# Four interleaved attention layers on one core: exponentials of two and two PSUM banks, later loads in pieces, a new written order

## The chip, the cores and the metric

The kernel runs on one core of a Trainium2 chip. The metric is the device time of one execution in microseconds (us), lower is better. TensorE is called PE here, VectorE DVE, ScalarE ACT, GpSimd POOL, SyncE SP; PEld are PE's weight loads.

## The reference

The input x has 2048 rows of 512 columns in bf16. Four layers follow each other, A, B, A, B, with the same weights for both A and for both B. Each adds its result to x, and each starts with a layernorm without scale.

```python
# A: 32 heads of 16, causal window of 256 rows
q, k, v = split(layernorm(x) @ wqkv)
scores = where(0 <= i - j < 256, q @ k.T * 0.25, -1e9)
x = x + concat(softmax(scores) @ v) @ wo
# B: 32 heads of 16, linear attention
phi = lambda t: where(t > 0, t + 1, exp(t)) + 1e-6
kv, z = phi(k).T @ v, sum(phi(k))
x = x + concat((phi(q) @ kv) / (phi(q) @ z + 1e-6)) @ wo
```

## The kernel before

Rows of x are cut into 16 tiles of 128, and four tiles make a block of 512. For a block, layer A computes transposed queries and keys (`q_unit`, `k_unit`, L711 to L742) and values (`v_unit`, L743), each by `proj` (L510): four matmuls of 128x512 into one bank of PSUM, followed by one evacuation. The values go through SBUF to SBUF DMAs on SP's queue (L757, four for each tile) into a layout in which two heads stand apart. Layer B of the same block follows as soon as the block is there: keys, values and queries (`bk_unit`, `bv_unit`, `bq_units`), a running sum over the blocks, and after the last block of a layer the normalizers (`norm_pair`, `norm_unit`) and the output products (`p2_tile`). PSUM has 8 banks of 128x512 f32, all held as one tile `psb`.

Attention is made of 152 score operations (`scores`, L762), 76 for each layer A. One of them is 8 to 12 small matmuls of 32 rows (L774), which fill four banks: banks 0, 1 and 2, and one of the banks 3 to 7. ACT then takes the exponential of three banks in one instruction of 128x1536 (L785) and of the fourth in one of 128x512 (L788). DVE or POOL masks the edges (L803, L808), and groups of 128x34 matmuls (L831) multiply with the values. Since banks 0 to 2 exist once, the score matmuls of the next operation wait until the exponential of L785 has read them.

Which instruction comes when on every engine isn't left to a scheduler. `ORDER` (L207) is a string of some 2,350 entries. An entry is the number of an operation, a letter for the engine (P for PE, A for ACT, V for DVE, G for POOL, S for SP, H for a landing in memory) and the buffers or banks that it takes. `Planner.run` walks over it and emits. Operations that several engines can do, such as masks, evacuations and the layernorm's factors, are given to one by the letter. An entry with F puts matmuls of the identity into a free bank (`fill`, L442), whose results nobody reads; there are 113 of them.

The rows 8 to 15 of x, and the weights woA, wB and woB, are loaded by five large DMAs that ACT issues between its exponentials (L1051 to L1056). At the start ACT and DVE zero the five buffers of the spread values (L499, L501). At the end a check of the normalizers is reduced to one flag (L886, L1307, L1311), all engines read it (L1312), and a branch leads to a safe version that never runs with these inputs.

Of the kernel before, what the change touches and what calls it, by code (L numbers as in the profile page):

```python
# [9 lines left out]
ACT = mybir.ActivationFunctionType  # L10
# [7 lines left out]
P = 128  # L18
D = 512
# [5 lines left out]
VW = 17  # L25

# [93 lines left out]

class Planner:
# [22 lines left out]
    def run(self):  # L144
# [7 lines left out]
        ahead = {"P": 9, "A": 1, "V": 9, "G": 1}  # L152
        marks = {}
        for e, k in ahead.items():
            marks.setdefault([i for i, x in enumerate(plan) if x[1] == e][-k], []).append(engine[e])
        for i, (n, e, places) in enumerate(plan):
            for m in marks.get(i, ()):
                self.tc.mark_branch_hint_location("safe", "LikelyTaken", [getattr(mybir.EngineType, {"ACT": "Activation", "POOL": "Pool"}.get(m, m))])
# [54 lines left out]
109P 110P 107V 111P 112V 129P04 130A 292P6 293V 287P7 288V 66P5 67V 30A 31H 144P03 145A 297P6 298V 318P7 319V 320S 301P5
131A 132G 133G 146A 149P06 150A 311P7 548V0 127V 116V 134P4 139P3 135P 302V 560V1 151A 152V 549G 550V00 552V2 561G 553G
155P05 156A 136P 137P 312V 138V 140P 141P 157A 147G 159G 142P 160P06 161A 162A 164G 163V 303P5 175P07 176A 143V 554V1
555S 321P4 322V 323S 304V 305P6 153G 158G 306V 180P03 177A 181A 299P4 300V 556V0 154G 148G 165P7 166P 182A 170P5 186P06
167P 187A 178G 171P 172P 173P 188A 174V 562V1 168P 191P03 169V 185G 557G 551S 184G 324P4 192A 190G 183G 558V2 559S 563S
325V 189V 326S 193A 194G 2F6 327P05 328A 329A 825V0 307P6 308V 3F4 332P03 333A 195G 179G 201P7 202P 196P5 197P 203P 198P
199P 200V 821V1 209S0 334A 336G 337P04 338A 339A 204P 205V 569P6 341G 331V 1F5 342P03 343A 344A 822G 13V 571V 313P5 3F7
348P04 349A 579P7 330V 314V 350A 340G 353G 345G 3F3 364P03 365A 366A 346V 347V 581V 352V 206S1 351V 570V 817V2 369P04  # L220
371A 370A 215S2 212S3 335G 359P5 360P 361P 354P6 362P 363V 367G 818G 819V02 820S 26A 27H 355P 356P 357P 234V 580V 374P03
372V 829V2 375A 376A 378V 377G 368G 584P5 3F4 379P04 380A 585V 823V1 358V 381A 373G 830G 383G 826G 382G 309P7 3F3 385P03
386A 207P5 310V 384V 831V0 832S 586S 387A 390V 389V 388G 572P6 573V 401P04 402A 208V 574P7 575V 391P3 392P 393P 406P06
827V2 396P5 403A 404V 407A 397P 394P 398P 399P 408A 410G 576V 218V0 411P04 395V 412A 216P7 217V 230V1 413A 415G 219G
409G 405V 3F6 416P03 417A 418A 419G 420V 567P6 3F7 422P04 423A 568V 400V 414G 421G 424A 426V 425V 587P7 588V 589S 824S
213P3 438P05 439A 427G 2F6 433P6 434P 428P7 443P04 440A 444A 445A 447G 429P 430P 431P 435P 432V 436P 437V 442V 220V01
221S 448P05 449A 582P7 450A 451G 8V 446V 214V 828S 3F6 453P04 454A 564P6 566V 441V 452V 455A 456G 458G 457G 3F5 459P03
460A 593P5 565V 594V 461A 462V 463V 590P4 595S 591V 592S 596P06 597A 598A 464G 465P5 466P 467P 601P03 602A 468P 470P6
471P 603A 231G 472P 473P 606P04 605G 469V 599V 474V 604V 583V 607A 608A 609V 210P5 3F6 611P03 612A 610G 837P6 838V 613A
614V 616V 615G 600G 3F7 617P04 618A 833P7 834V 619A 620G 622V 621V 3F6 633P03 634A 475S1 476P6 232V0 477V 487V0 488G 28A  # L230
29H 478S0 623P7 484S2 211V 624P 638P04 639A 625P 626P 481S3 628P6 629P 630P 631P 640A 642G 643P05 644A 627V 226V1 849P7
850V 851S 635A 645A 647G 641G 636G 632V 852P4 853V 854S 648P07 839P3 649A 577P5 578V 650A 653V 646V 651V 840V 654P04
637V 655A 656A 658V 657V 489G10 652G 490S 479P6 485P5 670P07 671A 659G 2F3 665P4 666P 667P 672A 675P03 676A 673G 222V0
223G 224G1 668P 660P7 661P 662P 486V 663P 664V 680P05 480V 677A 681A 858P3 499V2 859V 225S 233S 860S 679V 669V 491V0
682A 684G 227G 683V 2F7 685P06 686A 687A 855P7 856V 3F5 691P03 692A 674V 689V 678V 693A 696V 695V 847P5 482P6 228G2 229S
690G 688G 707P04 708A 483V 694G 2F7 697P7 698P 702P6 709A 712P03 703P 713A 699P 700P 704P 705P 706V 717P04 714A 718A
495V1 496G 497G0 719A 721G 835P3 836V 701V 710V 848V 716V 2F6 722P06 723A 498S 724A 727V 725V 845P3 2F7 728P04 729A 500G
846V 492G 711G 726V 730A 267P5 3F7 861P06 862A 863A 275P7 276A 732V 715V 731G 720V 733G 734P4 735P 866P03 867A 739P6
740P 741P 277V 278V 736P 737P 738V 744S0 268A 747S1 857S 742P 872P07 743V 750S2 868A 871G 269V 870G 493G0 494S 873A
841P4 842V 270V 874A 875V 501G1 3F6 877P03 878A 843P6 879A 882G 844V 869V 3F7 883P04 884A 745P5 746V 3F6 897P03 865V  # L240
885A 886V 876G 748P5 749V 760V0 898A 864G 887P6 888P 902P04 889P 890P 880V 881V 756V1 757G 899A 758G02 903A 904A 751P5
752V 764V2 503V 891V 908P03 909A 239P70 240V 906G 910A 912G 235P50 236A 237V 913P04 914A 900G 892P3 893P 894P 895P 896V
915A 917V 918G 905V 238V 2F6 919P06 920A 921A 901G 502S 532P7 544P4 545A 951P03 952A 916G 911G 922V 907G 1F5 923P5 924P
928P6 546V 953A 547V 533A 925P 926P 927V 956P04 957A 955G 954G 958A 960G 961G 761G 929P 930P 931P 932V 534V 535V 263P5
264A 962P03 963A 245P61 246V 933P70 934V 253P42 254V 265V 266V 964A 967P06 969A 968A 753S1 754P7 241P61 242A 755V 768V1
769G 970G 249P52 250A 973P03 974A 972G 975A 243V 244V 251V 762G1 937P71 938V 252V 271P4 272A 965V 273V 274V 935P6 936V
247P7 987P05 989A 988A 990G 966V 976G 959G 255P30 504P51 505A 506V 248V 256A 259P40 260A 508P61 257V 258V 509A 759S
939P7 941A01 942G 940V 261P6 262V 763S 765A 507V 766V1 767S 992P03 994A 946V2 514P40 510P60 522P52 977P7 978P 979P 993A
997V 971G 995G 511A 980P 981V 943A 515A 512V 513V 523V 996G 991G 998P03 1000A 999A 518P42 944P7 519A 982P3 983P 984P
516P6 517V 1003P05 1005A 1004A 985P 986V 947A 524P60 773P51 1001V 520G 521V 1002V 945V 525A 526V 527V 770G1 528P30 529A  # L250
774A 775V 776V 1009P04 1010A 1011A 777P71 778A 530P6 536P3 779P50 780A 531V 787P62 771S 537A 788A 789V 790V 781V 782V
1012G 1013P7 1006G 1007G 538G 1008G 783P40 784A 1014P 1015P 1016P 1017V 791P62 785P5 786V 539V 948G 772V 1018P4 1019P
1020P 1021P 1022V 1041V 949P5 950A 793P70 1027P00 1028V 1023P11 809P5 794A 795V 796V 1024A 1029P0 1030V 1036A0 1025P1
# [75 lines left out]
def build(ctx, tc, A_x, A_wqkv, A_wo, B_x, B_wqkv, B_wo, out, force_safe=False):  # L329
# [95 lines left out]
    def fast_network(ctx_f):  # L425
# [934 lines left out]
```

## Time and profile before

| what | us |
|---|---|
| median of 3 timed runs | 447.42 |
| lowest and highest of them | 446.45 and 449.89 |
| the profiled execution's own time | 445.83 |
| its span, first to last instruction | 444.1 |

The profiled execution is 1.6 us under the median, and its span leaves 1.7 us around it. Busy time is the share in which an engine has an instruction in work; the records of two instructions that follow each other on ACT, DVE or PE can overlap, since one begins to read while the other still writes. Matmuls are pipelined: a 128x512 matmul has a record of 0.38 us, while the next starts after 0.22 us.

### The profile page before, as it was taken

The numbers are of one execution on the slowest core, as the hardware profiler recorded it, in microseconds if no ns is written. First come the engines' busy times: TensorE is split into PE (matmuls) and PEld (weight loads), VectorE is DVE, ScalarE is ACT, GpSimd is POOL, SyncE is SP. The second block draws the span as 40 slices with busy tenths as digits, with TensorE's granted clock in tenths as the row PEclk, the third lists the DMA queues.
The fourth block names the chain that finished last, engine by engine and source line by source line (L and its number), as shares of the span: only waits on it lengthen the run. The fifth ranks groups of instructions, "written<-read, shape, count | busy, mean of one in ns | idle before, by whom it ended". The sixth has DMA issues, their size and how long they took to land.

```text
span 444.1 us, 15303 instructions
## 1 busy us (share of the span) xinstructions
PE 423.7 (95%) x6307; PEld 223.3 (50%) x6307; DVE 367.3 (83%) x874; ACT 374.1 (84%) x474; POOL 219.7 (49%) x485
## 2 busy tenths in 40 slices
PE   7989989999999999999999999999999989999995
PEld 2346545555554646554344465554555555565332
DVE  6899897878677787768996988989887969789985
ACT  6879999999999999667689999999899989984631
POOL 5436555325554645523763374564255558543332
PEclk9999999999999999999999999999999999999999
DMA  7421331234203100001011015223511221100014
GB/s 235 134 76 33 79 85 27 51 69 139 50 17 65 35 13 15 13 3 49 0 39 30 18 23 86 38 27 63 74 38 40 39 38 27 38 3 2 2 47 146
DMA packets 54330, 22.27 MB, mean 50 GB/s; under 512 B 38384, under 2 KB 53744, under 8 KB 54256
## 3 DMA queue, kind: packets, MB, share of 16 engines
q1 hardware_dynamic: 49760, 16.80, 18.6%
q10 hardware_dynamic: 4496, 4.46, 3.5%
q8 instruction: 50, 0.82, 0.8%
q14 instruction: 24, 0.20, 0.1%
HBM read 6.29 MB, written 2.10 MB: 19 GB/s over the span
## 4 chain that ended last, share of the span: by engine, by line
PE 57%; DVE 16%; POOL 9%; ACT 7%; issue 6%; DMA 4%; SPq 1%; DVEq 0%; POOLq 0%; ACTq 0%
PE psb L520 32%; PE psb L831 11%; PE psb L774 7%; POOL pt L808 4%; ACT pt L785 3%; PE psb L444 3%; DVE pt L803 3%; DMA xnT<-xn 2%; ACT pt L788 2%; DVE pks L899 2%; DVE pqT L1037 1%; PE psb L539 1%; PE psb L1033 1%; POOL xn L607 1%; DVE vst L507 1%
## 5 line engine op out<-in xcount | busy, mean ns | idle before, releaser
L785 ACT ACTIVATE pt<-psb 128x1536 bf16<-128x1536 f32 (+1 forms) x152 | 218.2, 1435 | 18.8 <-PE psb L774 17.1
L808 POOL TENSOR_SCALAR_AFFINE_SELECT pt<-pt 128x256 bf16<-128x256 bf16 x274 | 113.6, 443 | 120.3 <-ACT pt L788 113.6
L788 ACT ACTIVATE pt<-psb 128x512 bf16<-128x512 f32 (+1 forms) x152 | 89.6, 593 | 2.0 <-PE psb L774 1.5
L831 PEld LDWEIGHTS <-pt 128*128 128x128 bf16 x2880 | 81.3, 96 | 18.0 <-issue 6.5
L831 PE MATMUL psb<-vbd,pt 128*128 128x34 bf16 x2880 | 86.5, 178 | 3.3 <-DVE qT L507 1.1
L520 PE MATMUL psb<-xnT,wA 128*128 128x512 bf16 x256 | 64.7, 380 | 1.6 <-DVE vst L507 0.8
L803 DVE TENSOR_TENSOR pt<-pt,tri 128x256 bf16<-128x256 bf16 (+1 forms) x149 | 55.1, 394 | 12.1 <-ACT pt L788 11.7
L774 PE MATMUL psb<-qT,kall 32*128 32x320 bf16 (+4 forms) x1568 | 60.7, 246 | 3.0 <-ACT pt L785 2.5
L520 PE MATMUL psb<-wB,xnT 128*128 128x512 bf16 x256 | 61.6, 380 | 1.6 <-DMA xnT<-xn 1.2
L520 PEld LDWEIGHTS <-xnT 128*128 128x128 bf16 x384 | 34.1, 97 | 41.8 <-issue 4.7
L774 PEld LDWEIGHTS <-kall 32*128 32x128 bf16 x1568 | 25.8, 92 | 45.6 <-issue 40.6
L520 PEld LDWEIGHTS <-wA 128*128 128x128 bf16 x256 | 21.9, 97 | 29.3 <-issue 9.1
L444 PE MATMUL psb<-identb 128*128 128x512 bf16 x113 | 33.0, 401 | 2.3 <-POOL identb L372 1.5
L520 PE MATMUL psb<-woA,oT 128*128 128x512 bf16 x128 | 32.7, 381 | 0.6 <-DMA oT<-o_sb 0.6
L520 PE MATMUL psb<-wA,xnT 128*128 128x512 bf16 x128 | 32.5, 380 | 0.5 <-DMA xnT<-xn 0.3
L520 PE MATMUL psb<-xnT,wB 128*128 128x512 bf16 x128 | 32.3, 380 | 0.0
L726 DVE TENSOR_TENSOR kall<-psb,eo 128x1024 bf16<-128x1024 f32 x24 | 29.1, 1213 | 3.3 <-PE psb L520 2.2
L520 PE MATMUL psb<-wkv,pqT 128*128 128x512 bf16 x128 | 30.4, 380 | 0.1
L845 DVE TENSOR_TENSOR o_sb<-psb,rall 128x256 bf16<-128x256 f32 x64 | 27.2, 424 | 2.4 <-DMA oT<-o_sb 0.2
L844 DVE RECIPROCAL rall<-psb 128x16 f32<-128x16 f32 x64 | 15.9, 249 | 15.8 <-PE psb L831 15.5
L641 DVE BATCH_NORM_STATS2 ln_st<-xres 128x6 f32<-128x512 f32 (+1 forms) x39 | 26.7, 684 | 1.4 <-DMA xres<-in_A_x_dram 1.0
L893 ACT ACTIVATE pks<-psb 128x512 bf16<-128x512 f32 x32 | 19.2, 603 | 5.9 <-PE psb L520 5.8
(126 smaller groups left out, 532.5 us busy)
## 6 DMA issues: line engine op xcount, KB each, us to landing
vbd<-vst SPq DMA_DIRECT2D x128, 34.0 KB, 1.9
out_dram<-ost SPq DMA_DIRECT2D x16, 128.0 KB, 1.8
xres<-in_A_x_dram ACTq DMA_DIRECT2D x1, 1024.0 KB, 6.0
wB<-in_B_wqkv_dram ACTq DMA_DIRECT2D x1, 1024.0 KB, 5.5
xnT<-xn SPq DMA_TRANSPOSE x40, 2.7
wA<-in_A_wqkv_dram SPq DMA_DIRECT2D x1, 512.0 KB, 6.8
xres<-in_A_x_dram SPq DMA_DIRECT2D x1, 512.0 KB, 8.0
wB<-in_B_wqkv_dram ACTq DMA_DIRECT2D x1, 512.0 KB, 3.8
```

Of the source, the lines that this page charges most:

```text
L444: nc.tensor.matmul(psb[:, k, :], lhsT=identb[:], rhs=identb[:].unsqueeze(1).to_broadcast([P, NCT, P]), start=True, stop=True)
L520: nc.tensor.matmul(t["t"][:], lhsT=lhs(c), rhs=rhs(c), start=(c == 0), stop=(c == NCT - 1))
L641: nc.vector.bn_stats(t["st"][:], x())
L726: nc.vector.tensor_tensor(kall[:, r0:r0 + 2, t, :, :, :].rearrange("p r m k h -> p r (m k) h"), ps().rearrange("p (r c) -> p r c", r=2).un ...
L774: nc.tensor.matmul(psb[:, sT.k + x if x < 3 else sS.k, at * 64:(at + w) * 64], lhsT=kbd[half(m)][32 * x:32 * x + 32, tt, m % 4, :, :], rhs ...
L785: nc.scalar.activation(body[:, 0:3, 0:w_all, :], psb[:, 0:3, 0:w_all * 64].rearrange("p x (s c) -> p x s c", c=64), ACT.Exp, scale=0.25)
L788: nc.scalar.activation(body[:, 3, 0:w_all, :], psb[:, sS.k, 0:w_all * 64].rearrange("p (s c) -> p s c", c=64), ACT.Exp, scale=0.25)
L803: nc.vector.tensor_tensor(v, v, mt, op=ALU.mult)
L808: nc.gpsimd.affine_select(out=v, in_=v, compare_op=ALU.is_ge, fill=0.0, base=1 if kind == 0 else -2, pattern=[[0, 4], [2 * sg, 64]], chann ...
L831: nc.tensor.matmul(t["O"][:, x, g, :, :], lhsT=parts[b][0][:, s0:s0 + 2, :], rhs=vbd[half(m)][:, m % 4, :, 4 * tt + g, :], start=(n == 0), ...
L845: nc.vector.tensor_tensor(o_sb[:, u0:u0 + nu, P * tt:P * tt + P].rearrange("p u (h e) -> p u h e", e=DH), Ov[:, :, :, 0:DH], r.to_broadcas ...
L893: nc.scalar.activation(dst(), ps()[:], ACT.Exp)
```

## The change

- **Exponentials.** The four banks of a score operation are split two and two: banks 0 and 1, and one of the pairs 2-3, 4-5, 6-7. Both exponentials have 128x1024 elements.
- **Loads.** The later parts of x come two tiles at a time, and the weights in halves of 256 columns. SP issues them instead of ACT, each at its place in the order.
- **Start.** POOL zeroes the five value buffers; before, ACT did two and DVE three. `spread` gets a second copy with zeros, and the block mask `bd`, f32 before, is bf16.
- **Normalizers.** The matmuls of `norm_unit` read all 128 rows of `hl`, against weights that are zero in the half that isn't meant; before, they read 64 rows at a tile position of their own.
- **End.** The flag is computed within the written order, ahead of the last outputs. Outputs can be put by ACT as well as SP (nine by ACT). The last tile of the order (tile 2) is computed and put in two halves of 256 columns.
- **Order.** All of `ORDER` is new; the program has 50 fill matmuls.

```diff
-            sT, sS = Slot(rings["ps"], 3, (0,)), Slot(rings["ps"], 1, (3, 4, 5, 6, 7))
+            sT, sS = Slot(rings["ps"], 2, (0,)), Slot(rings["ps"], 2, (2, 4, 6))
...
-                            psb[:, sT.k + x if x < 3 else sS.k, at * 64:(at + w) * 64],
+                            psb[:, sT.k + x if x < 2 else sS.k + x - 2, at * 64:(at + w) * 64],
...
-                nc.scalar.activation(body[:, 0:3, 0:w_all, :], psb[:, 0:3, 0:w_all * 64].rearrange("p x (s c) -> p x s c", c=64), ACT.Exp, scale=0.25)
+                nc.scalar.activation(body[:, 0:2, 0:w_all, :], psb[:, 0:2, 0:w_all * 64].rearrange("p x (s c) -> p x s c", c=64), ACT.Exp, scale=0.25)
...
-                nc.scalar.activation(body[:, 3, 0:w_all, :], psb[:, sS.k, 0:w_all * 64].rearrange("p (s c) -> p s c", c=64), ACT.Exp, scale=0.25)
+                nc.scalar.activation(body[:, 2:4, 0:w_all, :], psb[:, sS.k:sS.k + 2, 0:w_all * 64].rearrange("p x (s c) -> p x s c", c=64), ACT.Exp, scale=0.25)
...
-        for b, t, c, fn in ((b_x[8:NT], 15.0, 3.0, lambda e: load_x(nc.scalar, 8, NT - 8)),
-                            ([B("woA")], 19.0, 1.5, lambda e: nc.scalar.dma_start(woA[:], wcols(A_wo, 0))),
-                            ([B("wB", 1)], 22.0, 3.0, lambda e: nc.scalar.dma_start(wB[:, :, D:3 * D], wcols(B_wqkv, 1, 2))),
-                            ([B("wB", 0)], 27.0, 1.5, lambda e: nc.scalar.dma_start(wB[:, :, 0:D], wcols(B_wqkv, 0))),
-                            ([B("woB")], 70.0, 1.5, lambda e: nc.scalar.dma_start(woB[:], wcols(B_wo, 0)))):
+        def part(w, src, which, k):
+            return lambda eng: eng.dma_start(w[:, :, which * D + 256 * k:which * D + 256 * k + 256], wcols(src, which)[:, :, 256 * k:256 * k + 256])
+        for i in range(8, NT, 2):
+            load(b_x[i:i + 2], 11.0, lambda eng, i=i: load_x(eng, i, 2))
+        for k in range(2):
+            load([B("woA", k)], 14.0, part(woA, A_wo, 0, k))
+        for which in (1, 2, 0):
+            for k in range(2):
+                load([B("wB", which, k)], 18.0, part(wB, B_wqkv, which, k))
...
-                    nc.tensor.matmul(t["p"][:, n, :], lhsT=spread[r0:r0 + 64, 2 * j + n, :, :], rhs=hl[I // 2][r0:r0 + 64, :],
-                                     start=True, stop=True, tile_position=(r0, 0))
+                    nc.tensor.matmul(t["p"][:, n, :], lhsT=spread[:, I % 2, 2 * j + n, :, :], rhs=hl[I // 2][:], start=True, stop=True)
...
+            if final and i == LAST:
+                ost = slot("xn")
+                for k in range(2):
+                    c = slice(256 * k, 256 * k + 256)
+                    o, s, ps = proj(lhs, lambda n, c=c: rhs(n)[:, c], reads=reads, deps=deps, use=use, n=256)
...
+                if a == 1:
+                    nc.vector.tensor_reduce(vall, vflags, axis=AX.X, op=ALU.min)
...
 ORDER = """
-6G 5G 0G 2G 7V 14H 1G 3G 17H 4G 50A0 35V0 36G 15H 16H 45V1 46G 40V2 37V10 47V2 10F1 38P0 39A 9A 51V 41G 42V3 52P1 53V
...
```

Three places of the order follow. The first is ACT at the first exponentials of the program (`pt` are the exponentials' buffers, `vst` and `qT` evacuated values and queries), first before, then now.

```order
L507 CAST vst_137<-psb 128x32x16
L785 ACTIVATE pt_146<-psb 128x3x512
L788 ACTIVATE pt_146<-psb 128x512
L785 ACTIVATE pt_147<-psb 128x3x512
L358 DMA xres<-in_A_x_dram 128x8x512
L785 ACTIVATE pt_148<-psb 128x3x448
L788 ACTIVATE pt_147<-psb 128x512
```

```order
L584 ACTIVATE ln<-ln 128x1
L810 ACTIVATE pt_145<-psb 128x2x512
L813 ACTIVATE pt_145<-psb 128x2x512
L810 ACTIVATE pt_146<-psb 128x2x512
L813 ACTIVATE pt_146<-psb 128x2x512
L813 ACTIVATE pt_147<-psb 128x2x448
L810 ACTIVATE pt_147<-psb 128x2x448
```

Three banks and one have become two and two, and the load is gone from ACT. The second place is SP's queue in the first third of the program (`vbd<-vst` are the four DMAs of a tile of values), before and now.

```order
L358 DMA xres<-in_A_x_dram 128x4x512
L757 DMA vbd_138<-vst_136 64x272 x4
L757 DMA vbd_138<-vst_137 64x272 x4
L757 DMA vbd_139<-vst_136 64x272 x4
L757 DMA vbd_139<-vst_137 64x272 x4
L757 DMA vbd_140<-vst_136 64x272 x4
L757 DMA vbd_140<-vst_137 64x272 x4
L530 DMA_TRANSPOSE xnT<-xn 128x4x128
```

```order
L363 DMA xres<-in_A_x_dram 128x4x512
L782 DMA vbd_137<-vst_135 64x272 x4
L782 DMA vbd_137<-vst_136 64x272 x4
L363 DMA xres<-in_A_x_dram 128x2x512
L782 DMA vbd_138<-vst_135 64x272 x4
L782 DMA vbd_138<-vst_136 64x272 x4
L363 DMA xres<-in_A_x_dram 128x2x512
L1089 DMA woA<-in_A_wo_dram 128x4x256
L363 DMA xres<-in_A_x_dram 128x2x512
L782 DMA vbd_139<-vst_135 64x272 x4
```

Six loads of the fourteen now stand among the first eight tiles of values on SP's queue. The third place is SP at the end (`ost` are output tiles), before and now.

```order
L530 DMA_TRANSPOSE xnT<-xn 128x4x128 x5
L757 DMA vbd_140<-vst_136 64x272 x4
L697 DMA out_dram<-ost 128x512 x16
L1312 TENSOR_LOAD vint
L1312 ISA x2
L1313 COMPARE_AND_BRANCH
```

```order
L722 DMA out_dram<-ost 128x512 x4
L1346 TENSOR_LOAD verdict
L1346 ISA x2
L722 DMA out_dram<-ost 128x512 x3
L698 DMA out_dram<-ost 128x256
L1347 COMPARE_AND_BRANCH
```

SP reads the flag ahead of its last four outputs, and half of the outputs have left its queue.

## Rows read from the trace of the kernel before

**Rows 1.** The page, part 1: busy time, share of the span, instructions.
```profile
PE 423.7 (95%) x6307; PEld 223.3 (50%) x6307; DVE 367.3 (83%) x874; ACT 374.1 (84%) x474; POOL 219.7 (49%) x485
```

**Rows 2.** Stretch, length, busy PE, PEld, DVE, ACT, POOL; granted clock; DMA share, GB/s.
```profile
0.00:13.00 13.00, 10.03 (x49) 4.03 (x53) 9.44 (x31) 8.91 (x13) 6.57 (x28) 1.00 0.65 202
13.00:182.40 169.40, 161.49 (x2690) 89.07 (x2691) 138.71 (x324) 157.20 (x181) 84.91 (x200) 1.00 0.26 59
182.40:227.00 44.60, 43.70 (x441) 20.89 (x439) 35.25 (x89) 28.29 (x60) 21.60 (x32) 1.00 0.07 18
227.00:395.00 168.00, 164.27 (x2734) 88.94 (x2733) 142.94 (x348) 158.93 (x185) 90.73 (x207) 1.00 0.23 40
395.00:423.40 28.40, 27.98 (x329) 13.72 (x328) 26.13 (x64) 16.54 (x32) 9.56 (x15) 1.00 0.01 2
```

**Rows 3.** Timeline of ACT, 69 to 73 us: start, duration, instruction, idle time before it.
```profile
69.67 1.45 ACT L785 ACTIVATE pt<-psb 128x1536 bf16<-128x1536 f32 x1 [0.45 <-PE psb L774]
71.02 0.59 ACT L788 ACTIVATE pt<-psb 128x512 bf16<-128x512 f32 x1
71.62 1.45 ACT L785 ACTIVATE pt<-psb 128x1536 bf16<-128x1536 f32 x1
```

**Rows 4.** Timeline of PE in the same stretch.
```profile
69.56 1.69 PE L831 MATMUL psb<-vbd,pt 128*128 128x34 bf16 x60
71.18 0.40 PE L774 MATMUL psb<-qT,kall 32*128 32x320 bf16 x8
71.51 1.04 PE L520 MATMUL psb<-woA,oT 128*128 128x512 bf16 x4
72.39 0.81 PE L444 MATMUL psb<-identb 128*128 128x512 bf16 x3
73.13 0.40 PE L774 MATMUL psb<-qT,kall 32*128 32x64 bf16 x12
```

**Rows 5.** Groups by line and shape, whole span: busy, mean ns, idle before.
```profile
L785 ACT ACTIVATE pt<-psb 128x1536 bf16<-128x1536 f32 x136 | 197.5, 1452 | 16.5 <-PE psb L774 15.1
L788 ACT ACTIVATE pt<-psb 128x512 bf16<-128x512 f32 x136 | 81.2, 599 | 2.0 <-PE psb L774 1.5 <-ACT pqT L893 0.5
```

**Rows 6.** Busy time of L444, the fill matmuls, in the two A stretches.
```profile
13.00:182.40 169.40, 20.13 (x72) 6.79 (x72) 1.00 0.26 59
227.00:395.00 168.00, 6.66 (x24) 2.26 (x24) 1.00 0.23 40
```

**Rows 7.** Timeline of PE around the start and in the tail.
```profile
9.37 1.02 PE L520 MATMUL psb<-xnT,wA 128*128 128x512 bf16 x4
12.92 0.40 PE L774 MATMUL psb<-qT,kall 32*128 32x192 bf16 x8
427.77 1.03 PE L1033 MATMUL psb<-hl,spread 64*128 64x512 bf16 x4
428.74 1.90 PE L520 MATMUL psb<-wkv,pqT 128*128 128x512 bf16 x8
```

**Rows 8.** Timeline at 15 and at 22 us: a load on ACT's queue, DVE's work.
```profile
15.53 0.37 ACTq L358 DMA_DIRECT2D xres<-in_A_x_dram  x1
22.09 0.69 DVE L507 CAST vst<-psb 128x512 bf16<-128x512 f32 x1 [1.42 <-DMA vbd<-vst]
24.38 1.87 DVE L499 MEMSET vbd<- 128x2176 bf16 x1 [0.40 <-issue]
```

**Rows 9.** DMA issues, 14 to 24 us: size, time to landing.
```profile
xres<-in_A_x_dram ACTq DMA_DIRECT2D x1, 1024.0 KB, 6.0
vbd<-vst SPq DMA_DIRECT2D x11, 34.0 KB, 3.3
```

**Rows 10.** Timeline of DVE at the end.
```profile
439.57 0.69 DVE L695 TENSOR_TENSOR ost<-psb,xres 128x512 bf16<-128x512 f32 x1 [0.23 <-PE psb L883]
...
440.60 0.14 DVE L1311 CAST vint<-vall 1x1 int32<-1x1 f32 x1
```

**Rows 11.** The page, part 3: instruction packets, their MB and share.
```profile
q8 instruction: 50, 0.82, 0.8%
```

More of the change, by code (lines that the diff above doesn't have):

```diff
@@ L25 @@
 VW = 17
+LAST = 2
 RA = [(1, 1, 5), (-3, 0, 2), (-4, 0, 1)]
@@ L151, in run @@
         plan = re.findall(r"(\d+)([PAVGSHF])(\d*)", ORDER)
-        ahead = {"P": 9, "A": 1, "V": 9, "G": 1}
         marks = {}
[L154 to L158, printed above, removed]
+        for e, k in AHEAD.items():
+            marks.setdefault([at for at, x in enumerate(plan) if x[1] == e][-k], []).append(ENGINES[e])
+        for at, (n, e, places) in enumerate(plan):
+            for m in marks.get(at, ()):
+                self.tc.mark_branch_hint_location("safe", "LikelyTaken", [m])
             if e == "F":
@@ L213 @@
[L213 to L217, printed above, removed]
@@ L508, in evac, with proj @@
             return pl.op({"DVE": .685, "ACT": .59}, f_evac, reads=reads, writes=writes, deps=deps, use=[take_slot] + list(use))
-        def proj(lhs, rhs, reads=(), deps=(), use=(), take=(), pre=None, frees=()):
+        def proj(lhs, rhs, reads=(), deps=(), use=(), take=(), pre=None, frees=(), n=D):
             deps = list(deps) + [d for b in frees for d in b.r + b.w]
@@ L517, in fn @@
                     pre()
-                t["t"] = psb[:, s.k, :]
+                t["t"] = psb[:, s.k, 0:n]
                 for c in range(NCT):
                     nc.tensor.matmul(t["t"][:], lhsT=lhs(c), rhs=rhs(c), start=(c == 0), stop=(c == NCT - 1))
-            o = pl.op({"PE": .863}, fn, reads=reads, deps=deps, take=[s] + list(take), use=use, kind="proj")
+            o = pl.op({"PE": .863 * n / D}, fn, reads=reads, deps=deps, take=[s] + list(take), use=use, kind="proj")
             return o, s, (lambda: t["t"])
@@ L675, in out_rows, with f_part, f_put @@
             t = {}
+            if final and i == LAST:
[3 more added lines that the diff above has]
+                    o, s, ps = proj(lhs, lambda n, c=c: rhs(n)[:, c], reads=reads, deps=deps, use=use, n=256)
+                    def f_part(e, k=k, c=c, ps=ps):
+                        if k == 0:
+                            t["o"] = work.tile([P, D], BF, name="ost", tag=f"xn{ost.k}", bufs=1)
+                        nc.vector.tensor_tensor(t["o"][:, c], ps(), xres[:, i, c], op=ALU.add)
+                    r = pl.op({"DVE": .355}, f_part, reads=[B("x", i)], deps=[o] if k == 0 else [o, r], use=[s] if k == 0 else [s, ost], take=[ost] if k == 0 else ())
+                    def f_put(e, c=c):
+                        (nc.sync if e == "SP" else nc.scalar).dma_start(o_dram[i][:, c], t["o"][:, c])
+                    pl.op({"SP": .4, "ACT": .45}, f_put, reads=[B("verdict")], deps=[r], use=[ost], kind="put")
+                return
             o, s, ps = proj(lhs, rhs, reads=reads, deps=deps, use=use)
@@ L696, in out_rows @@
                     r = pl.op({"DVE": .684}, fe, reads=[B("x", i)], deps=[o], use=[s], take=[ost])
-                pl.op({"SP": .4}, lambda e: nc.sync.dma_start(o_dram[i], t["o"][:]), deps=[r], use=[ost])
+                pl.op({"SP": .4, "ACT": .45}, lambda e: (nc.sync if e == "SP" else nc.scalar).dma_start(o_dram[i], t["o"][:]), deps=[r], use=[ost], kind="put")
             else:
@@ L963, in bq_units @@
                 ps.append(proj(lambda c, t=t: wB[:, c, t * P:(t + 1) * P], lambda c: X["t"][:, c, :],
-                               reads=[B("wB", 0)] + [B("xq", 4 * I + u) for u in range(4)], deps=lastq + before))
+                               reads=[B("wB", 0, t // 2)] + [B("xq", 4 * I + u) for u in range(4)], deps=lastq + before))
                 lastq[:] = [ps[t][0]]
```

332 lines of the change are left out of this document (175 added, 157 removed).

## The prediction

> **What bounds the kernel now.** The page's first part comes first: PE is busy for 95% of the span, ACT for 84%, DVE for 83%, POOL for 49% [rows 1]. A share of busy time can't say which of the first three sets the pace, so the span is cut at its stages next [rows 2]: a start of 13 us, the first A of 169.4 us, a B of 44.6 us, the second A of 168.0 us, and the rest, 49.1 us, which is the last B and the outputs. In the two B stretches PE is busy for 43.70 of 44.60 us and 27.98 of 28.40 us, and ACT for little over half: there PE alone is the wall, and nothing but less work on PE shortens them. In the two A stretches ACT is busy for 157.20 of 169.40 us and 158.93 of 168.00 us, and PE for about as much. A part of PE's time there is no work: 72 and 24 of the matmuls are fills, 20.13 and 6.66 us of records [rows 6], or at 0.216 us from one start to the next 15.5 and 5.2 us. So in A it is ACT, or the loop in which ACT and PE wait for each other.
>
> The timeline shows that loop. On ACT the exponential of three banks begins at 69.67 us, that of one bank at 71.02, the next three banks at 71.62: a period of 1.95 us [rows 3]. On PE the score matmuls start at 71.18, 0.06 us after the first of these exponentials has ended (69.67 + 1.45 = 71.12), last 0.40 us, and the next exponential follows at 71.62 [rows 3, 4]. 1.45 + 0.06 + 0.40 + 0.04 = 1.95: the round trip over banks 0 to 2 alone makes the period, with nothing to spare. ACT alone would need less. Its records overlap by 0.10 us (71.12 against 71.02), so a pair costs it 1.452 + 0.599 - 0.20 = 1.85 us [rows 5]. Where PE is later than the end of the large exponential, ACT also stands idle, as the 0.45 us in front of 69.67 [rows 3]: all waits of this kind are 16.5 us in front of the large shape [rows 5].
>
> **The change part by part**, against the profiled execution's 445.83 us.
>
> *Exponentials, two and two.* By rows 5 a bank more costs (1452 - 599) / 2 = 427 ns, so two banks cost 1026 ns, and a pair 2 x 1026 - 200 = 1.85 us, as before: ACT's own work is unchanged. The round trip becomes 1.026 + 0.06 + 0.40 + 0.04 = 1.53 us, which leaves PE 0.32 us of play per operation. How much of this counts depends on PE's work between two score operations, which I counted along PE's order in both programs, at 0.216 us for a 128x512 matmul (fills included), 0.025 us for a 128x34 one (60 in 1.69 us, less the 0.18 us tail of a record), 0.056 us for a transpose and 0.33 us for a score operation (71.18 to 71.51) [rows 4]. Before, 75 intervals of the first A hold 146.5 us and 75 of the second 151.3 us. If an interval takes 1.95 us or PE's work, whichever is more, the sums are 158.5 and 156.6 us; the two stretches from first to last score operation are some 166.8 us each, so 8 to 10 us on top are ACT's other work and late operands. In the changed program the intervals hold 136.3 and 147.2 us of PE work. They are less even: 13 and 24 of them exceed 2.17 us (9 and 10 before). Two bounds follow. If PE can use the play each time (1.85 + 0.32 = 2.17 us until ACT waits), the sums are 75 x 1.85 + 11.2 = 150.0 and 138.8 + 11.1 = 149.9 us, 15 us less than before together. If long intervals follow each other and the play is used up, an interval takes 1.85 us or PE's work, 157.1 and 161.8 us, together 4 us more. I take -9 us, nearer to the first, since most long intervals stand next to one of 1.2 to 1.6 us (one `proj` or half of one product group and the score operation). ACT's other work between the exponentials stays: 26 and 29 instructions of about 0.6 us now, 22 and 29 before.
>
> *Fill matmuls.* 63 are gone, 63 x 0.216 = 13.6 us of PE time, 44 of them in the first A stretch and 19 in the second, where PE waited anyhow. They are in the count above, and have no term of their own. The granted clock was 1.00 in every A and B stretch, the level of 2.4 GHz [rows 2].
>
> *Start.* PE's first projections begin at 9.37 us and the first score operation at 12.92, after four groups of four [rows 7]. Now six groups stand ahead of it: 2 x 0.87 = +1.7 us, since in front of the scores nothing hides them. What it buys is in the intervals. The load of 1 MB at 15.53 us takes 6.0 us to land, and the value DMAs of that stretch take 3.3 us [rows 8, 9]; DVE waits 1.42 us for one [rows 8]. In pieces of 256 KB the waiting behind a load is a quarter as long. The three zeroings on DVE (1.87 us each) leave an engine that is late there [rows 8]. Together -2 us, with bounds of -5 us (the 1.42 us wait and two zeroings) and +2 us: six more issues on SP among the first values, of 0.37 us each [rows 8].
>
> *Later loads.* ACT loses five issues of 0.37 us; they stand beside its exponentials in the trace [rows 8], so this is 0, at most -1.9 us. SP's queue is idle for long parts of A, and takes the other eight at no cost.
>
> *Normalizers.* Four of the 64-row matmuls take PE 0.97 us (427.77 to 428.74) where four of the full height take 0.86 [rows 7]. 32 of them give -0.9 us, in stretches where PE is the wall. *End.* After the last output tile on DVE (from 439.57) come the flag's operations until 440.74 us [rows 10]; 0.5 us of them go, and half a tile (0.69 / 2) is less to wait for. The end still waits for the last output to land, so -0.5 us.
>
> The sum: -9 + 1.7 - 2 - 0.9 - 0.5 = -10.7 us, from 445.83 to 435.1 us. The profiled execution lay 1.6 us under the median of 447.42, so some of that comes on top: I forecast 435.5 us as a median, 2.7% less.
>
> The order was also searched for instruction fetches. The page shows 50 instruction packets [rows 11], and no row puts a wait down to one, so my sum has nothing for it. The Trainium skill says in "Runtime: NRT & Kernel Launch", section "Instruction fetch mechanics", that an engine fetches ahead in blocks of 16 KiB and that the cost of crossing one is mostly hidden. The packets agree with the block (0.82 MB in 50), and by that rule this part of the change is worth nothing.
>
> **The rivals.** *The play is used up (no change).* PE's longer intervals follow each other in the second A, where its work is 147.2 us in 75 intervals. Then the two A stretches cost 4 us more instead of 9 less: 445.8 + 4 + 1.7 - 3.4 = 448 us. For it speaks that PE is as busy there as ACT [rows 2]; against it that the waits of today come from intervals barely over 1.95 us, which now have room.
>
> *ACT becomes the only wall (much faster).* With 0.32 us of play and the fills gone ACT could run its pairs without gaps: 76 x 1.85 plus its other work of some 13 and 15 us is 153 and 156 us, against 169.4 and 168.0. That is 28 us less, less 1.7 us at the start: 419 us. Against it: PE holds 147 us in the second A, and two engines that wait for each other don't both run at 95%.
>
> *SP's queue turns into the wait (slower).* The loads now stand among the value DMAs, which the products wait for, and DVE's next evacuation of values behind them [rows 8]. Each of the six early loads puts 0.37 us of issue and, if SP also waits for the landing of a load before it goes on, up to a quarter of 6.0 us in front of the values: 6 x 1.9 = 11 us. It decides once the values of a block come more than about 3 us late, which is what the block's other work hides. With the gain of the exponentials halved: 445.8 + 11 - 4.5 + 1.7 - 1.4 = 452.6 us.
>
> *The clock (slower).* The fills go, PE idles more in the first A (its intervals hold 136.3 us of work now, 146.5 before), and the granted clock could fall to 1.2 GHz. If it does so for a tenth of the two A stretches, 28 us of PE work there takes 28 us longer: over 460 us. Against it: the second A kept 1.00 with a third of the first's fills [rows 2, 6].
>
> **How the numbers follow.** The forecast gets 0.63, with a range of its own from 428 to 442 us (the -9 us between -15 and -3, and the start). The used-up play gets 0.14, ACT as the only wall 0.15, SP's queue 0.06, the clock 0.02. The range for 8 in 10 runs from 425 to 446 us: it leaves out the lower half of the fast rival and the slower rivals. A measurement of this kernel can tell about 1% from no change, that is 442.9 and 451.9 us. Faster by over 1%: nearly all of the forecast and the fast rival, 0.77. Within 1%: the used-up play and a remnant, 0.15. Slower by over 1%: 0.08.
>
> **What would show it.** Right: the idle time of ACT in front of the first exponential of a pair falls from 16.5 us to under 8; the period in an undisturbed stretch falls from 1.95 to 1.85 us; the A stretches shorten by 4 to 5 us each and the B stretches by under 1 us. Wrong: A stretches of 167 us or more with ACT waiting for the score matmuls (the play is used up); value or transpose DMAs that end the waits of DVE or PE (SP's queue); a granted clock under 1.00; or B stretches that change by several us, which nothing above explains.

## The result and the profile after

The changed kernel takes 436.67 us as a median of four runs (435.30 to 437.30), the kernel before beside it 447.43 us. The ratio is 0.9749, with an interval of 0.9709 to 0.9788: 2.5% faster. The forecast was 435.5 us, 2.7%. The profiled execution took 437.04 us, with a span of 435.3.

The page's first part and the stretches between the first and the last exponential of each A (columns as in [rows 1] and [rows 2], whose bounds were slightly wider):

```profile
PE 409.6 (94%) x6248; PEld 221.3 (51%) x6248; DVE 351.8 (81%) x839; ACT 371.8 (85%) x496; POOL 225.4 (52%) x506
```
```profile
0.00:15.00 15.00, 11.85 (x63) 5.05 (x64) 10.32 (x36) 6.87 (x17) 9.14 (x29) 1.00 0.61 184
15.00:176.50 161.50, 152.17 (x2633) 85.34 (x2634) 127.24 (x305) 154.58 (x184) 89.28 (x219) 0.99 0.28 64
176.50:219.40 42.90, 42.83 (x441) 21.41 (x440) 35.66 (x87) 29.66 (x66) 15.54 (x23) 1.00 0.03 6
219.40:385.70 166.30, 160.44 (x2719) 88.93 (x2718) 139.59 (x335) 158.30 (x189) 92.19 (x215) 1.00 0.21 40
```

Cut the same way, at the first and last exponential of each A, the kernels stand as follows. The last two columns are runs of the next section, which keep one half of the change each (of two runs each the faster, 448.91 and 465.15 us).

| stage, us | before | after | new order, three and one | old order, two and two |
|---|---|---|---|---|
| to the first exponential | 13.5 | 15.0 | 15.4 | 15.0 |
| first A | 168.9 | 161.5 | 166.4 | 180.0 |
| between the two (B) | 44.6 | 42.9 | 42.9 | 44.9 |
| second A | 168.2 | 166.3 | 172.2 | 175.8 |
| from the last exponential | 49.0 | 49.6 | 49.5 | 49.2 |
| span | 444.1 | 435.3 | 446.4 | 464.9 |

The first A gave 7.4 us, the second 1.9, B 1.7; the start cost 1.5 and the tail 0.6. The sum is -8.8 us between the two spans. The medians differ by 2 us more, since the profiled execution lay under its median before (445.83 against 447.4) and a little over it after.

The loop of [rows 3, 4] after the change, ACT first, then PE:

```profile
64.31 1.02 ACT L810 ACTIVATE pt<-psb 128x1024 bf16<-128x1024 f32 x1
65.23 1.02 ACT L813 ACTIVATE pt<-psb 128x1024 bf16<-128x1024 f32 x1
66.14 1.03 ACT L810 ACTIVATE pt<-psb 128x1024 bf16<-128x1024 f32 x1
```
```profile
65.41 0.40 PE L799 MATMUL psb<-qT,kall 32*128 32x192 bf16 x8
65.74 1.04 PE L532 MATMUL psb<-xnT,wA 128*128 128x512 bf16 x4
66.61 0.59 PE L453 MATMUL psb<-identb 128*128 128x512 bf16 x2
```

The first exponential ends at 65.33, the score matmuls run from 65.41 to 65.81, and ACT takes the next pair at 66.14, when it is through with the last one: a period of 1.83 us where it was 1.95, and 0.33 us in which the scores lie ready. Groups by shape, to be held against [rows 5], and PE's score group:

```profile
L810 ACT ACTIVATE pt<-psb 128x1024 bf16<-128x1024 f32 x136 | 142.0, 1044 | 9.8 <-PE psb L799 7.8 <-PE psb L908 1.0
L813 ACT ACTIVATE pt<-psb 128x1024 bf16<-128x1024 f32 x136 | 141.8, 1048 | 0.8 <-DVE xn L605 0.2
```
```profile
L799 PE MATMUL psb<-qT,kall 32*128 32x320 bf16 (+4 forms) x1568 | 61.9, 247 | 9.2 <-ACT pt L810 5.6 <-DVE vst L519 0.6
```

ACT's idle time in front of the large shape fell from 16.5 to 9.8 us. A pair costs ACT 2.09 us by its means, 0.04 more than the 2.05 of before.

### The profile page after: what moved, and what is told of

It is laid out like the page before. It is cut to its first block, busy times and chain, and to the rows that moved or that the text cites. A ratio compares the mean times of both kernels' runs of the same rounds, so it can differ in the third digit from the quotient of the medians.

```text
span 435.3 us, 15188 instructions
## 1 busy us (share of the span) xinstructions
PE 409.6 (94%) x6248; PEld 221.3 (51%) x6248; DVE 351.8 (81%) x839; ACT 371.8 (85%) x496; POOL 225.4 (52%) x506
## 4 chain that ended last, share of the span: by engine, by line
## 5 line engine op out<-in xcount | busy, mean ns | idle before, releaser
L833 POOL TENSOR_SCALAR_AFFINE_SELECT pt<-pt 128x256 bf16<-128x256 bf16 x293 | 119.0, 437 | 106.8 <-ACT pt L813 83.8
L810 ACT ACTIVATE pt<-psb 128x1024 bf16<-128x1024 f32 (+1 forms) x152 | 156.9, 1032 | 11.4 <-PE psb L799 9.2
L813 ACT ACTIVATE pt<-psb 128x1024 bf16<-128x1024 f32 (+1 forms) x152 | 156.4, 1036 | 0.8 <-DVE xn L605 0.2
L799 PE MATMUL psb<-qT,kall 32*128 32x320 bf16 (+4 forms) x1568 | 61.9, 247 | 9.2 <-ACT pt L810 5.6
L532 PE MATMUL psb<-wB,xnT 128*128 128x512 bf16 x256 | 62.8, 379 | 1.3 <-DVE pqT L930 0.6
L799 PEld LDWEIGHTS <-kall 32*128 32x128 bf16 x1568 | 28.9, 92 | 53.7 <-issue 46.6
L828 DVE TENSOR_TENSOR pt<-pt,tri 128x256 bf16<-128x256 bf16 (+1 forms) x135 | 49.7, 392 | 4.8 <-ACT pt L813 3.8
L532 PE MATMUL psb<-wkv,pqT 128*128 128x512 bf16 (+1 forms) x132 | 30.0, 373 | 0.3 <-DVE ost L720 0.2
L652 DVE BATCH_NORM_STATS2 ln<-xres 128x6 f32<-128x512 f32 (+1 forms) x39 | 26.6, 682 | 1.8 <-DMA xres<-in_A_x_dram 1.4
L924 ACT ACTIVATE pqT<-psb 128x512 bf16<-128x512 f32 x32 | 19.4, 622 | 6.9 <-PE psb L532 6.8
L930 DVE SCALAR_TENSOR_TENSOR pqT<-psb,pqT 128x512 bf16<-128x512 f32 x32 | 22.0, 687 | 0.7
```

Source lines behind the costliest of these rows:

```text
L532: nc.tensor.matmul(t["t"][:], lhsT=lhs(c), rhs=rhs(c), start=(c == 0), stop=(c == NCT - 1))
L652: nc.vector.bn_stats(t["st"], x())
L799: nc.tensor.matmul(psb[:, sT.k + x if x < 2 else sS.k + x - 2, at * 64:(at + w) * 64], lhsT=kbd[half(m)][32 * x:32 * x + 32, tt, m % 4, :, :],
L810: nc.scalar.activation(body[:, 0:2, 0:w_all, :], psb[:, 0:2, 0:w_all * 64].rearrange("p x (s c) -> p x s c", c=64), ACT.Exp, scale=0.25)
L813: nc.scalar.activation(body[:, 2:4, 0:w_all, :], psb[:, sS.k:sS.k + 2, 0:w_all * 64].rearrange("p x (s c) -> p x s c", c=64), ACT.Exp, sca ...
L828: nc.vector.tensor_tensor(v, v, mt, op=ALU.mult)
```

## The experiments

Every ratio is against the kernel before, run beside it; the changed kernel stands at 0.9749. The runs were spread over several chips, on which the kernel before had medians from 446.97 to 447.93 us; where two runs are compared by their medians, a difference of about 1 us can come from that.

**The new order without the split.** Row orders of all engines are kept. As the score tile now needs three neighbouring banks and one, the PSUM tiles had to be dealt to banks again; in the first run so that no two live tiles share one.

```diff
-            sT, sS = Slot(rings["ps"], 2, (0,)), Slot(rings["ps"], 2, (2, 4, 6))
+            sT, sS = Slot(rings["ps"], 3, (0,)), Slot(rings["ps"], 1, (3, 4, 5, 6, 7))
...
-100P04 101A 84P3 102A 104G 105P06
+100P05 101A 84P6 102A 104G 105P04
```

> The changed kernel, every engine's row order kept, with the score tile cut into three banks and one again. Theory 1: the split carries the gain, so it is lost: +9 us on the changed kernel, 445 to 447 us, the first A stage back at 167 us or more. Theory 2: the order carries it: 437 to 440 us, the first A stage at 161 to 164 us. If both are needed: 440 to 445 us.

Measured: 468.24 us, ratio 1.0464 [1.0424, 1.0504], outside all three cases. The dealing itself could be the reason, so the run was repeated with each tile in the bank that had been read out longest ago:

```diff
-100P05 101A 84P6 102A 104G 105P04
+100P06 101A 84P4 102A 104G 105P05
```

> The run before on the new order with the score tile cut into three banks and one (468 us) again, row orders as there, but every PSUM tile dealt to the bank that was read out longest ago, so that no matmul waits for a bank that another choice would have had free. Theory A, the dealing made that run slow and the split is worth what the prediction says: 444 to 447 us. Theory B, the dealing made it slow and the order alone carries the gain: 435 to 439 us. Theory C, the new order does not stand three and one whatever the banks: 460 us or more, with over 20 us of TensorE waiting for the first exponential.

Measured: 448.91 us, 1.0054 [1.0030, 1.0078], 2 us above theory A and far from the other two. The control deals the changed kernel's own two and two by the same program:

> A control for the dealing: the changed kernel, orders and split unchanged, with its PSUM tiles dealt to banks by the same program that dealt those of the three-and-one run on the new order (448.9 us); 481 of 705 tiles change their bank. If the dealing costs nothing, 435 to 438 us, and the 12 us of that run are the split's. If the dealing costs by itself, 441 us or more, and that much has to be taken off.

Measured: 437.42 us, 0.9765 [0.9724, 0.9806], level with the changed kernel. So that dealing costs nothing where it could be checked, with two and two; with three and one it was not checked by itself. On the new order the split is then worth 448.91 - 436.67 = 12.2 us (13.6 by the two ratios); the new order without it, with everything else of the change, is worth nothing (0.5% slower). Where the 12 us lie is in PE's score group of that run:

```profile
L799 PE MATMUL psb<-qT,kall 32*128 32x320 bf16 (+4 forms) x1568 | 60.6, 246 | 28.0 <-ACT pt L810 25.2 <-DVE kall L751 0.4
```

PE waits 25.2 us for the exponential of three banks, in the changed kernel 5.6 us for that of two. Both A stretches pay: 166.4 and 172.2 us against 161.5 and 166.3.

**The split on the old order.** Again every engine's own row order is kept, and the banks are dealt so that pairs stay free, first without regard to time, then with it. So that each tile finds its banks free, the entries of different engines also had to be shifted against each other, in the same way in both runs.

```diff
-            sT, sS = Slot(rings["ps"], 3, (0,)), Slot(rings["ps"], 1, (3, 4, 5, 6, 7))
+            sT, sS = Slot(rings["ps"], 2, (0,)), Slot(rings["ps"], 2, (2, 3, 4, 5, 6))
```

> The kernel before, every engine's row order kept, with the score tile cut into two and two banks (the banks of the other PSUM tiles are dealt out anew so that pairs stay free). Theory 1, the prediction's: the split alone carries the gain, about -9 us (438 us), 4 to 5 us from each A stage, ScalarE's idle time ahead of the first exponential falls from 18.8 us to about 10. Theory 2, the gain needs the new order: within 2 us of before (445 to 449 us), because in the old order the next score operation is late for other reasons and the idle time of ScalarE stays at 16 us or more. Theory 3, the play is used up: slower by about 4 us.

Measured: 480.31 us, 1.0727 [1.0686, 1.0767]; none of the theories had it.

```diff
-            sT, sS = Slot(rings["ps"], 2, (0,)), Slot(rings["ps"], 2, (2, 3, 4, 5, 6))
+            sT, sS = Slot(rings["ps"], 2, range(7)), Slot(rings["ps"], 2, range(7))
```

> The first run (the split into two and two on the old order, 480 us) again, with the banks dealt by time: any neighbouring two banks for either half, and every tile put where the last reader was through longest ago. Theory 1: the split alone carries the gain and only the dealing hid it: 438 us or so. Theory 2, the old order keeps so many other PSUM tiles open beside the score tiles that no dealing leaves a free pair in time: 455 to 465 us, with ScalarE idle ahead of its first exponential for more than in the kernel before (18.8 us), since the score operation comes late. Theory 3: between the two, 442 to 450 us, the split gains what the shortage takes.

Measured: 465.15 us, 1.0390 [1.0348, 1.0432], at the upper edge of theory 2. On the old order the split makes the kernel 18 us slower under the better dealing. In the profiled execution the granted clock fell to 0.50 three times ahead of the tail (at 8.6, 25.6 and 66.6 us), but that is little of the 18 us: the one run at a mean clock of 1.000 still took 462.75 us. The score group and ACT's exponentials, and then a place on PE and on ACT where it happens:

```profile
L774 PE MATMUL psb<-qT,kall 32*128 32x320 bf16 (+4 forms) x1568 | 71.0, 248 | 7.4 <-ACT pt L788 4.0 <-ACT pt L785 1.0 <-DVE o_sb L845 0.6
```
```profile
L785 ACT ACTIVATE pt<-psb 128x1024 bf16<-128x1024 f32 x136 | 139.3, 1024 | 30.2 <-PE psb L774 28.5
```
```profile
106.49 0.40 PE L774 MATMUL psb<-qT,kall 32*128 32x192 bf16 x8
106.82 1.04 PE L520 MATMUL psb<-woA,oT 128*128 128x512 bf16 x4
107.69 0.76 PE L831 MATMUL psb<-vbd,pt 128*128 128x34 bf16 x24
108.38 0.81 PE L774 MATMUL psb<-qT,kall 32*128 32x256 bf16 x8
```
```profile
106.92 1.02 ACT L785 ACTIVATE pt<-psb 128x1024 bf16<-128x1024 f32 x1 [0.39 <-PE psb L774]
...
109.14 1.02 ACT L785 ACTIVATE pt<-psb 128x1024 bf16<-128x1024 f32 x1 [1.20 <-PE psb L774]
```

The score operation at 108.38 takes 0.81 us in place of 0.40: three of its matmuls have begun, the fourth starts 0.43 us later, when DVE has read out another tile (its residual addition, L706), and ACT waits 1.20 us behind it. Counted in the trace, there are 37 such stops of more than 0.18 us between two matmuls of L774, 15.3 us together; 24 of them (9.3 us) end with the second exponential of an operation before, 11 (4.5 us) with DVE's reading of another tile. The kernel before has 2 such places (2.2 us), the changed kernel 5 (4.3 us). So the score operations do wait for banks, inside themselves. Over the span the group is busy for 71.0 us, where it was 60.7 before.

Why the banks are short is argued and not shown. By the entries of the two orders, when a score operation takes its banks, other tiles (projections, products) hold two or three banks in 51 of 152 cases in the old order, and in 24 of 152 in the new. With four banks for itself and two that ACT is still reading, all eight are then taken. But the operations that meet two or three taken banks, a third of all, also bear only a third of the time added against the kernel before (6.7 of 18.8 us, from one operation's first exponential to the next), so this count alone does not single out where the time goes. A version of the old order with fewer open tiles was not tried, and neither was the old order with three and one under the same dealing; another dealing could give part of the 18 us back.

**Fills.** The kernel before without the 100 fill matmuls behind the first score operation, and the changed one without its 36; nothing reads what they write.

```diff
-117V 68P3 69V 291V0 3F6 118P04 86G
+117V 68P3 69V 291V0 118P04 86G
...
```

> The kernel before without the 100 fill matmuls behind the first score operation (21.6 us of TensorE at 0.216 us); they write nothing that is read. Theory 1, fills lie in time in which TensorE would wait anyway: within 2 us of before, ScalarE's idle time the same. Theory 2, they stood in the way of other matmuls: 3 to 13 us faster. Theory 3, they hold the clock: mean granted clock under 0.99, stretches at half speed behind idle time of TensorE, and slower by 3 us or more.

Measured: 444.45 us, 0.9918 [0.9886, 0.9949], 3.5 us faster, though the granted clock fell in one place (0.55 and 0.59 between 58 and 62 us). It fell behind 1.54 us of idle time of PE at 56.1 us; the kernel before has the same 1.54 us at 56.4 us, and its clock stayed at 1.00. PE's wait for the first exponential rose from 2.5 to 19.7 us: most of the 21.6 us of fills became waiting again, and the rest had been in the way.

> The changed kernel without the 36 fill matmuls behind the first score operation (7.8 us of TensorE); they write nothing that is read. Theory 1: 436 to 438 us, nothing changes. Theory 2, in the way: 431 to 435 us. Theory 3, they hold the clock: the stretch at half speed near 46 us grows or others appear, mean granted clock under 0.99, 439 us or more.

Measured: 435.62 us, 0.9730 [0.9682, 0.9778]: no difference from the changed kernel that can be told.

**The clock at 46 us.** The changed kernel's windows there, and PE's timeline:

```profile
44.00:46.00 2.00, 1.00 (x11) 0.43 (x11) 1.31 (x4) 2.00 (x4) 1.40 (x4) 0.92 0.41 66
46.00:48.00 2.00, 2.00 (x9) 0.56 (x11) 0.93 (x1) 1.55 (x2) 1.31 (x5) 0.50 0.36 70
48.00:50.00 2.00, 2.00 (x68) 1.64 (x60) 0.42 (x2) 1.54 (x2) 0.40 (x2) 0.73 0.31 61
```
```profile
43.34 0.38 PE L799 MATMUL psb<-qT,kall 32*128 32x320 bf16 x8
44.96 0.40 PE L799 MATMUL psb<-qT,kall 32*128 32x192 bf16 x8 [1.25 <-ACT pt L810]
45.40 1.63 PE L532 MATMUL psb<-xnT,wA 128*128 128x512 bf16 x4
```

PE idles for 1.25 us up to 44.96 us, and from 45.7 to 49.1 us the granted clock is at 0.50, the level of 1.2 GHz; four projections take 1.63 us instead of 1.02. The experiment puts five fills there:

```diff
-211A 213G 197G 345P04 346A
+211A 213G 197G 5F6 345P04 346A
```

> The changed kernel with five fill matmuls (1.08 us) ahead of the score operation that waits 1.25 us for ScalarE at 43.7 us. Theory 1, the idle time of TensorE there is what takes the granted clock to 0.50 behind it: no stretch under 0.9 between 44 and 50 us, 1.5 to 2.5 us faster (434 to 435 us). Theory 2, it is not the idle time, or the time lost there lies in play: the clock still falls, or 436 to 437.5 us all the same.

Measured: 435.25 us, 0.9742 [0.9711, 0.9772]. The clock stays at 1.00 up to the tail, and the runs' mean clock is 0.995 to 0.998 (0.992 to 0.998 without). The time gained, 1.4 us between the medians, is inside the intervals. So the idle time at this place is a part of the cause: the clock fell there in four of five profiled runs with the gap, and in none of the three with the gap filled. It is not the whole: in the run with whole loads below the clock stayed at 1.00 behind the same gap, and later in the changed kernel's own trace PE idles as long, in front of a score operation too, without any fall:

```profile
123.73 0.40 PE L799 MATMUL psb<-qT,kall 32*128 32x320 bf16 x12 [1.27 <-ACT pt L810]
```
```profile
122.00:124.00 2.00, 0.73 (x25) 0.43 (x24) 1.97 (x6) 2.00 (x4) 0.00 (x0) 1.00 0.00 0
124.00:126.00 2.00, 1.97 (x31) 0.90 (x20) 1.57 (x5) 2.00 (x3) 0.67 (x1) 1.00 0.00 0
```

All eight traces of the new order with two and two have these 1.27 us, and in none did the clock fall behind them. What else it takes stays open.

The next run keeps the five fills there and leaves out the others behind the first score operation but two.

> The changed kernel without its fill matmuls behind the first score operation but two, and with five ahead of the score operation at 43.7 us, where the granted clock fell. If fills elsewhere only cost (about 1 us in the run without any) and the clock is all that the gap costs (about 1.4 us in the run with five there), the two add: 434 to 435 us, no stretch under 0.9 before 425 us. If both were chance, 436 to 437 us. If the other fills had held the clock elsewhere, a stretch at 0.5 appears in another place, and 437 us or more.

Measured: 434.47 us (433.99 to 434.88), 0.9722 [0.9696, 0.9749], clock at 1.00 there. It is the lowest median of all, 2.2 us under the changed kernel (1.2 by the ratios), but the intervals overlap.

**The end.** ACT's last four issues in the changed kernel, and SP's last six in the run that moves all nine output issues of ACT to SP (the text below says eight):

```profile
428.60 3.17 ACTq L722 DMA_DIRECT2D out_dram<-ost  x4
```

```diff
-2260A
+2260S
...
-2308A
+2308S
```

> The changed kernel with the eight output transfers that it issues on ScalarE issued on SyncE, in the same place of the order. Theory 1, ScalarE's last four issues (0.34 to 1.53 us each, the last transfer landing at 433.39) set the end: 1 to 2 us faster, 435 us, the time from the last output matmul to the end back to some 4.6 us. Theory 2, the transfers themselves take that long, and SyncE's queue is as late: within 0.5 us, and SyncE's issues stand in a row instead. Theory 3: slower, since SyncE has other transfers to issue there.

```profile
428.46 2.58 SPq L722 DMA_DIRECT2D out_dram<-ost  x4
431.14 0.41 SPq L698 DMA_DIRECT2D out_dram<-ost  x1
431.59 0.45 SPq L722 DMA_DIRECT2D out_dram<-ost  x1
```

Measured: 437.10 us, 0.9773 [0.9737, 0.9809], no gain: SP's issues now stand in a row up to 432.04 us. Taking the issues off ACT does not bring the end forward.

**Loads.** The later loads in one piece each, on SP (x as shown, the weights likewise):

```diff
-            load(b_x[i:i + 2], 11.0, lambda eng, i=i: load_x(eng, i, 2))
+            load(b_x[i:i + 2], 11.0, lambda eng, i=i: load_x(eng, 8, NT - 8) if i == 8 else None)
```

> The changed kernel with its later loads in one piece each again (activations of tiles 8 to 15 in one transfer of 1024 KB, each weight in one of 512 KB), issued on SyncE where the first piece was. Theory 1, the prediction's: whole loads hold up the small transfers behind them, 1 to 3 us slower than the changed kernel, with TensorE or ScalarE waiting for a transfer between 15 and 30 us. Theory 2: the small transfers were hidden anyway, within 1 us.

Measured: 435.55 us, 0.9746 [0.9717, 0.9776]. The pieces are worth nothing that can be told. The transfers in pieces, from the page's part on DMA issues, are to be held against [rows 9] (1024 KB in 6.0 us); a quarter of the size takes half the time and not, as the prediction had it, a quarter:

```profile
xres<-in_A_x_dram SPq DMA_DIRECT2D x4, 256.0 KB, 3.0
```

Whole loads together with the gap filled and the other fills gone:

> The changed kernel with only the five and two fills at 43.7 us behind the first score operation (434.5 us by itself) and its later loads in one piece each (435.6 us by itself). If the two add: 433 to 434 us. If the loads' difference was chance: 434 to 435 us, as without them. If fewer transfers move the stalls: 436 us or more.

Measured: 435.12 us, 0.9722 [0.9690, 0.9755]. The two do not add; it came out as expected if the whole loads' difference was chance.

## Why the prediction was right, and where it was not

- *What bounds the kernel.* Right. The loop over the first exponential's banks is what the split shortens: with the new order held fixed, undoing the split brings 20 us of PE's waiting for it back (5.6 to 25.2), and 12.2 us of time.
- *The -9 us for exponentials and intervals.* Near as a sum: the two A stretches gave 9.3 us, where the forecast had 9, and 11 with the 2 us for loads and zeroings that it put into the same intervals. The parts of it came out as said: 1026 ns for two banks (1044 and 1048 as means, 1032 as the median), a period of 1.85 us (1.83), 0.32 us of play (0.33). But 4 to 5 us from each A was wrong: 7.4 and 1.9. By the prediction's bounds the first A was to change by -8.5 us (the play counts each time) to -1.4 (the play is used up), the second by -6.7 to +5.2. So the first lies near its better bound, and the second in the middle, as its fuller intervals (147.2 us of PE work against 136.3) would have had it. ACT's idle time fell to 9.8 us, not under 8.
- *The step that failed: the interval rule, taken without the banks.* The prediction gave an interval 1.85 us or PE's work and asked nothing of PSUM. By that rule the old order with two and two would have gained 7 to 26 us (counted as in the prediction, its intervals give 307.6 us at the worst and 289.5 at the best, against 315.1); it lost 18.7 in the A stretches, with score operations that stop for banks. The new order with three and one would have lost 11.7 (326.8 against 315.1); it lost 1.5. So the -9 holds two errors that cancel: by the rule the order costs 11.7 us, which leaves -20.7 to the split, where the runs show +1.5 and -10.8. To that extent its size is luck. That the new order spares the banks because it keeps fewer other tiles open, which the prediction never looked at, is likely and not shown.
- *Fills, no term of their own.* In the two A stretches of the changed kernel 28 and 5 are left, against 72 and 24 in [rows 6] (windows of the fill's line):

```profile
15.00:176.50 161.50, 8.65 (x28) 2.76 (x28) 0.99 0.28 64
219.40:385.70 166.30, 1.73 (x5) 0.49 (x5) 1.00 0.21 40
```

  The reason given, that PE waited there anyhow, holds for most of them: 100 fills cost the kernel before 3.5 us, so the 64 of them that went are worth some 2 us, an estimate by their share.
- *Start +1.7.* The first exponential comes 1.5 us later, behind six groups of projections on PE's timeline [rows 7]:

```profile
9.31 1.02 PE L532 MATMUL psb<-wA,xnT 128*128 128x512 bf16 x4 [0.23 <-DVE xnT L554]
...
14.58 0.40 PE L799 MATMUL psb<-qT,kall 32*128 32x192 bf16 x8
```

- *Loads in pieces and zeroings -2.* The loads' part is not there: whole loads take the same time. DVE's wait for the value DMAs [rows 8] is 1.3 us after, 1.4 before, and 0.8 with whole loads, so the pieces did not shorten it. The zeroings were not tested by themselves.
- *Normalizers -0.9.* Right: from one start to the next the 32 matmuls take 7.01 us in place of 8.04. On PE's timeline four of them need 0.87 us, in [rows 7] 0.97:

```profile
420.01 1.03 PE L1063 MATMUL psb<-hl,spread 128*128 128x512 bf16 x4
420.88 2.33 PE L532 MATMUL psb<-wkv,pqT 128*128 128x512 bf16 x12
```

- *End -0.5.* Wrong in sign. From the end of the last output matmul to the end of the span it was 4.6 us and is 6.2. The flag is out of the way, but eight outputs are issued between 426.8 and 431.8 us, and ACT's last four issues take 3.17 us together (one of them 1.53), where SP before needed 3.47 us for seven. DVE's last tiles, in the timeline:

```profile
428.80 0.69 DVE L720 TENSOR_TENSOR ost<-psb,xres 128x512 bf16<-128x512 f32 x1 [0.23 <-PE psb L532]
429.41 0.41 DVE L695 TENSOR_TENSOR ost<-psb,xres 128x256 bf16<-128x256 f32 x1
```

DVE is through at 429.82, where [rows 10] went on to 440.74, and the span ends 5.5 us behind it; before it ended 3.4 us behind the flag. With all issues on SP the end is as late, and one issue there takes 1.08 us; why some issues take so long stays open.
- *Instruction fetches, nothing.* The page's part on queues shows the same packets as [rows 11], as its row behind this paragraph says, and the order that was searched for them is, without the split, no faster. The runs don't isolate the fetches further.

```profile
q8 instruction: 50, 0.82, 0.8%
```

- *The rivals.* Used-up play shows in part, in the second A. ACT as the only wall did not come: its stretches were to fall to 153 and 156 us, and they stand at 161.5 and 166.3. The reason given against it fails all the same: in both stretches after the change PE and ACT are each busy for 94 to 97%, and in the second A of before they were at 98 and 95%. The clock rival came true on a small scale, in one stretch from 45.7 to 49.1 us. SP's queue did not turn into a wait. B gave 1.7 us where under 1 was said; the new order has it with three and one too (42.9 us), so it belongs to the order or the normalizers, and not to the split.

Loads and end erred the same way, by 2 us each. B, 1.2 us better than said, made up for some of it, so the spans differ by 8.8 us where the parts summed to 10.7. That the medians differ by 10.8 all the same comes from the 2 us by which the two profiled executions stand off their medians, and is luck too. Had the same split been forecast for the old order alone, the same reasoning would have missed by 26 us at the least.

## What to carry to other kernels

Count buffers as well as time: a split that frees banks earlier for one wait needs its banks in another pattern. Here it gave 12 us on one order and cost 18 on another, so test the split and the order each alone. When an order is kept but its tiles must move, deal the banks by when they were last read, and run a control, or the dealing is measured in place of the edit. Filling matmuls are not free in a loop where PE is nearly the wall (here 100 cost 3.5 us); put them, if anywhere, where the granted clock is seen to fall.

## What the runs showed of the hardware that was not expected

- The choice of PSUM banks alone, all row orders equal, moved the time by 19.3 us on the new order (468.24 to 448.91) and by 15.2 us on the old one (480.31 to 465.15). The Trainium skill, "Perfetto Trace Analysis", section "Matmuls", says that independent matmul groups should rotate through the banks, so that evacuating one overlaps the next. The runs fit it: in the slower of each pair a tile may go to a bank that has only just been handed back, in the faster one it goes to the bank read out longest ago.
- A wait inside a score operation shows only in part as idle time. In the old order with two and two the 37 stops of 15.3 us hold 6.3 us that the profile counts as idle; the group's busy time rose from 60.7 to 71.0 us.
- The granted clock fell to 0.50 behind 1.25 us of idle time of PE at 44 us, between stretches in which PE had been busy, and was back at 1.00 some 4 us later. In one of the five profiled runs with that gap it did not fall, and behind 1.27 us at 122 us it fell in none of eight.
